# A fixed TensorE order for the second expert, with the output row blocks in late groups between its products

## The chip, the cores and the metric

The kernel runs on one core of one Trainium2 chip. The metric is the device time of one execution in microseconds (us). The kernel before took 958.3 us, the median of three runs (957.17 to 958.48).

The engines are named as the profile names them: PE is TensorE (matrix products), PEld its weight loads, DVE is VectorE, ACT is ScalarE, POOL is GpSimd, and SP is the queue that issues most of the transfers.

## The reference

Attention with two kinds of masks is followed by two experts. Only the second expert matters here:

```
a = x @ w_a          # x: 2304 x 512, w_a and w_b: 512 x 1536
b = x @ w_b
return a * b @ w_out # w_out: 1536 x 512
```

## The kernel before

Attention and the first expert fill the first 538 us. They leave the second expert's input in DRAM, in blocks named `x2d`. Everything below is about the second expert, which fills the rest.

**Precision.** Each operand is split in a high and a low part, and each product is three matmuls (high by high, high by low, low by high). `parts` makes such a split: ACT casts the high part (line 150), and DVE or POOL subtracts it to get the low part (line 151).

**Steps.** The list `steps` has 18 entries. A step takes one group g of 768 rows (three groups) and one pair p of the 1536 hidden columns' blocks (six pairs). The order is p = 0, 1, 2 for g = 0, then for g = 1, then for g = 2, and then the same with p = 3, 4, 5. Steps are counted from one below: the change begins with the fourth (i = 3), which is g = 1 with p = 0.

**Products of a step.** For each of `w_a` (k even) and `w_b` (k odd) the step makes a 2 by 2 block product with seven instead of eight block multiplications. `products` returns the seven as functions. Each is six matmuls of 384 columns into one of three PSUM banks, X, Y and Z. With both k there are 14 slots, in the order X0 X1 Y0 Y1 X0 X1 Y0 Y1 Z0 Z1 Y0 Y1 Z0 Z1 (the digit is k % 2). A product that stands a second or third time in the list accumulates onto what the bank holds, so it may only start when the engines have read the state before it: X0 is first copied by ACT (`u1`, line 872) and then accumulated onto, and Y0 is first added to `u1` by DVE (line 866).

**Hidden blocks.** `hidden` multiplies a and b (DVE, line 899) and splits the result into a tile `hl` (ACT line 150, POOL line 151).

**Output row blocks.** `output` multiplies hidden blocks with `wo2` into a PSUM tile `o`, and there are two such tiles. After a block, DVE adds it to an accumulator in SBUF (line 940), or ACT copies it there for the first pairs (line 938). A block has 12 matmuls of 512 columns when it serves two pairs, and six when it serves one. After each step with p % 3 of 1 or 2, six blocks are put on the list `waiting`. The next step takes one of them at every second slot.

**Other work in the same steps.** Steps three, five, six, eight and nine also convert weights (`convert_forms`): load `raw`, ACT lines 137 and 142, DVE line 145 writing `z`, sums `zs` (lines 680 to 683), casts and subtractions into the single tile `forms`, and a store to `formd`. The first three steps and the tenth to twelfth convert `wo2` in the same way, with the tiles `z2`. The scheduler may run such work in a neighbouring step. At the first step of each group `x_forms` rebuilds the seven split inputs in the tiles `slab`. The `form` tiles, which hold converted weights, are loaded a step ahead (line 807) into four buffers.

**What sets the order.** The code gives the order in which instructions are recorded. A scheduler then orders each engine's instructions by its own estimate of when each is ready. So PE's row order is not that of the code: it interleaves matmuls of several products and several output blocks. `behind(list)` forbids one thing to the scheduler: an instruction may not be put ahead of those in the list on its engine.

Of the kernel before, what the change touches and what calls it, by code (L numbers as in the profile page):

```python
# [77 lines left out]
def fused_kernel(ctx: ExitStack, tc: tile.TileContext, qtl, ktl, vl, qs, ks, vs, cst, w1, w2, out):  # L78
# [5 lines left out]
    nc = tc.nc  # L84
# [85 lines left out]
    def run(steps):  # L170
        for f in steps:
            f()
# [317 lines left out]
    def tmp(name):  # L490
        return act.tile([128, NTB], F32, tag="t", name=name, bufs=NTMP)
# [4 lines left out]
    @contextmanager  # L496
    def behind(instructions):

        with ExitStack() as e:
            for i in instructions:  # L500
                e.enter_context(tc.issue_after(i))
            yield
# [227 lines left out]
    for t in range(NB):  # L730
# [10 lines left out]
        x = [xt[t, cc] for cc in range(NCC)]  # L741
        for fc in range(NFC):
# [34 lines left out]
            if t == 0:  # L777
                nc.vector.tensor_tensor(v, sg, v, op=ALU.mult)
                h = v
                made[:] = [nc.vector.scalar_tensor_tensor(h, th, 1.0, v, op0=ALU.add, op1=ALU.mult).ins]  # L780
            else:
                h = tmp("h")
# [23 lines left out]
    def load_forms(k):  # L806
        nc.sync.dma_start(flat(form_tile(k)), formd[k])
# [3 lines left out]
    def convert_wo2(fc):  # L811
# [14 lines left out]
        def last():  # L826
            w = wo2[fc] = []
            for q in (2 * (fc % 6), 2 * (fc % 6) + 1):
# [7 lines left out]
    PRODUCTS = [(1, 0, "X", True), (6, 4, "Y", True), (2, 1, "X", False), (5, 3, "Y", False),  # L836
                (7, 6, "Z", True), (3, 5, "Y", False), (4, 2, "Z", False)]

    def part():
        return p2b.tile([128, NTB], F32, tag="c", name="c", bufs=8)  # L840

    def products(g, k):

        st = {}
        w = forms.pop(k)
        x = dict(xf)
        banks = {}

        def bank(n):
            return banks[n][:, :NTB]  # L850

        def product(p, form, n, begins):
            def f():
                if begins:
                    banks[n] = psum.tile([128, 512], F32, tag=f"{n}{k % 2}", name=f"{n}{k % 2}")
                for c in range(2):
                    cs = slice(c * 128, (c + 1) * 128)
                    hi, lo = w[:, 0, form, cs], w[:, 1, form, cs]
                    nc.tensor.matmul(bank(n), hi, x[p][:, 0, c], start=begins and c == 0, stop=False, skip_group_check=not begins)  # L859
                    nc.tensor.matmul(bank(n), hi, x[p][:, 1, c], start=False, stop=False, skip_group_check=not begins)  # L860
                    nc.tensor.matmul(bank(n), lo, x[p][:, 0, c], start=False, stop=c == 1, skip_group_check=not begins)  # L861
                after(p)
            return f

        def plus(dst, a, n):
            nc.vector.tensor_tensor(dst, a, bank(n), op=ALU.add)  # L866
            return dst

        def after(p):
            if p == 1:  # L870
                st["u1"] = part()
                nc.scalar.copy(st["u1"], bank("X"))
            elif p == 6:
                st["u2"] = plus(part(), st["u1"], "Y")
            elif p == 2:
                if k % 2 == 0:
                    st["11"] = part()
                    if (g, k) == (0, 0):
                        nc.vector.tensor_copy(st["11"], bank("X"))
                    else:  # L880
                        nc.scalar.copy(st["11"], bank("X"))
                else:
                    st["11"] = bank("X")
            elif p == 5:
                st["u4"] = plus(part(), st["u1"], "Y")
            elif p == 7:
                st["22"] = plus(st["u4"], st["u4"], "Z")
            elif p == 3:
                st["12"] = plus(st["u1"], st["u1"], "Y")
            elif p == 4:  # L890
                st["21"] = plus(st["u2"], st["u2"], "Z")

        return st, [product(*p) for p in PRODUCTS]
# [3 lines left out]
    def hidden(p, a, b, c):  # L897

        nc.vector.tensor_tensor(a[c], a[c], b[c], op=ALU.mult)  # L899
        h = hl[p, c] = p2c.tile([128, 2, NTB], F32R, tag="h", name="hl", bufs=9)  # L900
        parts(a[c], h[:, 0], h[:, 1], nc.gpsimd)
# [5 lines left out]
    def acc_tile(j):  # L907
        acc[j] = slab[j][:, 3 * DM:] if j < 2 else slab[11][:, (j - 2) * DM:(j - 1) * DM]
        return acc[j]

    def output(g, ps, j, last=False):

        t, cols = j // NJ, slice(j % NJ * 128, j % NJ * 128 + 128)
        r0 = (2 * g + t) * NTB + j % NJ * 128
        chunks = [(p, i) for p in ps for i in range(2)]
        if last:
            for half, queue in enumerate((nc.sync, nc.scalar)):
                c = slice(half * 256, half * 256 + 256)
                o = psum.tile([128, 512], F32, tag="o", name="o", bufs=2)[:, :256]
                for n, (p, i) in enumerate(chunks):  # L920
                    h, w = hl[p, f"{i + 1}{t + 1}"], wo2[2 * p + i]
                    nc.tensor.matmul(o, h[:, 0, cols], w[0][:, c], start=n == 0, stop=False)
                    nc.tensor.matmul(o, h[:, 0, cols], w[1][:, c], start=False, stop=False)
                    nc.tensor.matmul(o, h[:, 1, cols], w[0][:, c], start=False, stop=n == len(chunks) - 1)
                nc.vector.tensor_tensor(acc[j][:, c], acc[j][:, c], o, op=ALU.add)
                queue.dma_start(out[r0:r0 + 128, c], acc[j][:, c])
            return
        o = psum.tile([128, 512], F32, tag="o", name="o", bufs=2)
        for n, (p, i) in enumerate(chunks):
            h, w = hl[p, f"{i + 1}{t + 1}"], wo2[2 * p + i]  # L930
            nc.tensor.matmul(o, h[:, 0, cols], w[0], start=n == 0, stop=False)  # L931
            nc.tensor.matmul(o, h[:, 0, cols], w[1], start=False, stop=False)  # L932
            nc.tensor.matmul(o, h[:, 1, cols], w[0], start=False, stop=n == len(chunks) - 1)  # L933
        while reload and (reload[0][1] != j or len(reload) > 1):
            again = reload.pop(0)
            nc.sync.dma_start(acc_tile(again[1]), accd[again])
        if ps[0] == 0:
            nc.scalar.copy(acc_tile(j), o)
        else:
            nc.vector.tensor_tensor(acc[j], acc[j], o, op=ALU.add)  # L940
        if ps[-1] == NP // 2 - 1:
            nc.sync.dma_start(accd[g, j], acc[j])
            if g == NB // 2 - 1:
                reload.append((0, j))
        if ps[-1] == NP - 1:
            nc.sync.dma_start(out[r0:r0 + 128, :], acc[j])
            if g + 1 < NB // 2:
                reload.append((g + 1, j))


    steps = [(ps, g, p) for ps in (range(0, 3), range(3, 6)) for g in range(NB // 2) for p in ps]
    converted = {2: [6], 4: [7], 5: [8, 9], 7: [10], 8: [11]}
    wo_ready = {0: (0, 1), 1: (2, 3), 2: (4, 5), 9: (6, 7), 10: (8, 9), 11: (10, 11)}
    waiting = []
    for i, (ps, g, p) in enumerate(steps):
        if i > 0 and p == ps[0]:
            for fs in x_forms(g).values():
                run(fs)
        ahead = []
        if i + 1 < len(steps):  # L960
            for k in (2 * steps[i + 1][2], 2 * steps[i + 1][2] + 1):
                if k not in forms:
                    ahead.append(lambda k=k: load_forms(k))
        for fc in wo_ready.get(i, ()):
            ahead += convert_wo2(fc)
        for k in converted.get(i, ()):
            ahead += convert_forms(k, False, True)
        a, pa = products(g, 2 * p)
        b, pb = products(g, 2 * p + 1)
        slots = [f for fs in zip(pa, pb) for f in fs]  # L970
        for n, f in enumerate(slots):
            f()
            run(ahead[len(ahead) * n // 14:len(ahead) * (n + 1) // 14])
            if waiting and n % 2:
                waiting.pop(0)()
            if n in (7, 9, 11):
                hidden(p, a, b, {7: "11", 9: "22", 11: "12"}[n])
        hidden(p, a, b, "21")
        if p % 3:
            js = (*range(NJ, 2 * NJ), *range(NJ)) if i + 1 == len(steps) else range(2 * NJ)  # L980
            waiting += [lambda g=g, q=(p - 1, p) if p % 3 == 1 else (p,), j=j, last=i + 1 == len(steps) and j == js[-1]:
                        output(g, q, j, last) for j in js]
# [70 lines left out]
```

## Time and profile before

| | |
|---|---|
| median of three runs | 958.3 us |
| the profiled execution | 957.71 us |
| its span in the trace | 955.9 us |
| granted TensorE clock, mean over the span | 0.989 |
| TensorE busy | 931.4 us, 97% |
| VectorE, ScalarE, GpSimd busy | 66%, 44%, 56% |
| second expert in the trace | from 538.5 us to the end |
| first instruction that the change moves | TensorE, 601.80 us |

The span is what the trace covers, and the profiled execution's own time is 1.8 us longer. Times in the rows are us from the span's start.

### The profile page before, as it was taken

The numbers are of one execution on the slowest core, as the hardware profiler recorded it, in microseconds if no ns is written. First come the engines' busy times: TensorE is split into PE (matmuls) and PEld (weight loads), VectorE is DVE, ScalarE is ACT, GpSimd is POOL, SyncE is SP. The second block draws the span as 40 slices with busy tenths as digits, with TensorE's granted clock in tenths as the row PEclk, the third lists the DMA queues.
The fourth block names the chain that finished last, engine by engine and source line by source line (L and its number), as shares of the span: only waits on it lengthen the run. The fifth ranks groups of instructions, "written<-read, shape, count | busy, mean of one in ns | idle before, by whom it ended". The sixth has DMA issues, their size and how long they took to land.

```text
span 955.9 us, 14129 instructions
## 1 busy us (share of the span) xinstructions
PE 931.4 (97%) x5324; PEld 883.1 (92%) x5324; DVE 628.9 (66%) x916; ACT 420.7 (44%) x791; POOL 539.5 (56%) x405
## 2 busy tenths in 40 slices
PE   5999999999999999999999999999999999999998
PEld 3798899999999999999999998999999999999997
DVE  5669977558818895987576468667655655464534
ACT  5987645344443433444555545436424422122110
POOL 3568956468749687969379545655634424123211
PEclk6899999999999999999999999999999999999999
DMA  9974385527534553532787975997993973863701
GB/s 343 407 290 153 107 295 170 166 93 235 159 105 153 172 183 109 175 134 67 260 345 290 359 274 221 384 417 277 372 372 124 349 290 129 289 242 148 261 32 67
DMA packets 57507, 215.55 MB, mean 225 GB/s; under 512 B 5984, under 2 KB 14816, under 8 KB 51808
## 3 DMA queue, kind: packets, MB, share of 16 engines
q1 hardware_dynamic: 57152, 214.00, 61.6%
q8 instruction: 42, 0.69, 0.3%
q10 hardware_dynamic: 288, 0.66, 0.2%
q14 instruction: 25, 0.20, 0.1%
HBM read 172.17 MB, written 42.47 MB: 225 GB/s over the span
## 4 chain that ended last, share of the span: by engine, by line
PE 67%; DMA 9%; POOL 8%; DVE 6%; issue 4%; ACT 4%; SPq 0%; POOLq 0%; DVEq 0%; ACTq 0%
PE o L933 5%; PE o L932 5%; PE o L931 5%; POOL prod L248 4%; PE Y L860 4%; PE Y L861 4%; PE Y L859 4%; DMA raw<-in_w 3%; DMA gv_raw<-in_w 3%; PE y L482 3%; PE g_ps L483 3%; PE y L481 3%; PE y L483 3%; PE g_ps L481 3%; PE g_ps L482 3%
## 5 line engine op out<-in xcount | busy, mean ns | idle before, releaser
L151 POOL TENSOR_TENSOR hl<-c,hl 128x384 fp32r<-128x384 f32 x72 | 77.2, 1072 | 183.8 <-ACT hl L150 177.2
L248 POOL TENSOR_TENSOR prod<-kv_t,qs_t 128x512 f32<-128x512 f32 (+12 forms) x57 | 106.8, 1897 | 20.8 <-DMA kv_t<-in_ks 14.6
L482 PE MATMUL y<-hl,wo 128*128 128x384 f32 x288 | 97.1, 341 | 3.4 <-DVE hl L507 2.4
L281 POOL TENSOR_TENSOR prod<-kv_t,S_t 128x512 f32<-128x512 f32 (+12 forms) x57 | 86.8, 1536 | 21.8 <-issue 8.2
L481 PE MATMUL v_ps<-xx,gv 128*128 128x384 f32 x288 | 97.1, 337 | 2.0 <-DVE sg L762 1.9
L481 PE MATMUL g_ps<-xx,gv 128*128 128x384 f32 x288 | 97.3, 338 | 0.9 <-DVE sg L766 0.9
L482 PE MATMUL v_ps<-xx,gv 128*128 128x384 f32 x288 | 97.6, 339 | 0.0
L483 PE MATMUL v_ps<-xx,gv 128*128 128x384 f32 x288 | 97.2, 338 | 0.0
L483 PE MATMUL g_ps<-xx,gv 128*128 128x384 f32 x288 | 96.9, 337 | 0.0
L482 PE MATMUL g_ps<-xx,gv 128*128 128x384 f32 x288 | 96.5, 336 | 0.0
L866 DVE TENSOR_TENSOR c<-c,Y 128x384 f32<-128x384 f32 x108 | 58.8, 550 | 56.0 <-PE Y L861 50.8
L483 PE MATMUL y<-hl,wo 128*128 128x384 f32 x288 | 94.0, 335 | 0.0
L284 DVE TENSOR_REDUCE xs_t<-prod 128x64 f32<-128x448 f32 (+17 forms) x57 | 85.7, 1518 | 11.1 <-POOL prod L281 10.0
L507 POOL TENSOR_TENSOR hl<-h,hl 128x384 fp32r<-128x384 f32 x58 | 62.9, 1084 | 49.1 <-ACT hl L506 49.0
L481 PE MATMUL y<-hl,wo 128*128 128x384 f32 x288 | 84.0, 342 | 1.8 <-ACT hl L506 1.8
L932 PE MATMUL o<-slab,hl 128*128 128x512 f32 x214 | 83.9, 393 | 0.0
L931 PE MATMUL o<-slab,hl 128*128 128x512 f32 x214 | 83.4, 390 | 0.0
L933 PE MATMUL o<-slab,hl 128*128 128x512 f32 x214 | 82.3, 394 | 0.0
L150 ACT CAST hl<-c 128x384 fp32r<-128x384 f32 x72 | 36.9, 513 | 102.8 <-DVE c L899 102.8
L860 PE MATMUL Y<-slab,form 128*128 128x384 f32 x216 | 72.4, 335 | 0.0
L861 PE MATMUL Y<-slab,form 128*128 128x384 f32 x216 | 72.4, 335 | 0.0
L859 PE MATMUL Y<-slab,form 128*128 128x384 f32 x216 | 72.4, 335 | 0.0
(150 smaller groups left out, 2462.1 us busy)
## 6 DMA issues: line engine op xcount, KB each, us to landing
form<-formd SPq DMA_DIRECT2D x32, 1792.0 KB, 10.5
wo<-wod SPq DMA_DIRECT2D x59, 512.0 KB, 4.0
raw<-in_w SPq DMA_DIRECT2D x40, 512.0 KB, 7.2
gv_raw<-in_w SPq DMA_DIRECT2D x32, 512.0 KB, 10.2
formd<-form SPq DMA_DIRECT2D x6, 1792.0 KB, 8.2
formd<-forms SPq DMA_DIRECT2D x6, 1792.0 KB, 12.6
slab<-x2d SPq DMA_DIRECT2D x24, 384.0 KB, 4.2
wod<-wo SPq DMA_DIRECT2D x12, 512.0 KB, 3.0
```

Of the source, the lines that this page charges most:

```text
L248: nc.gpsimd.tensor_tensor(pr, st["ks", g][:, :, :n, :], st["qs"][:, heads(g), mm:mm + 1, :].to_broadcast([128, G, n, D]), op=ALU.mult)
L281: st["pvm"] = nc.gpsimd.tensor_tensor(pr, st["vs", g][:, :, :n, :], st["S"][:, heads(g), mm, :n, None].to_broadcast([128, G, n, D]), op=AL ...
L284: st["pvr"] = nc.vector.tensor_reduce(st["xs"][:, mm, heads(g), :], pr.rearrange("p g n d -> p g d n"), axis=X, op=ALU.add)
L481: nc.tensor.matmul(out_ps, w_hi, x_hi, start=start, stop=False)
L482: nc.tensor.matmul(out_ps, w_hi, x_lo, start=False, stop=False)
L483: nc.tensor.matmul(out_ps, w_lo, x_hi, start=False, stop=stop)
L859: nc.tensor.matmul(bank(n), hi, x[p][:, 0, c], start=begins and c == 0, stop=False, skip_group_check=not begins)
L860: nc.tensor.matmul(bank(n), hi, x[p][:, 1, c], start=False, stop=False, skip_group_check=not begins)
L861: nc.tensor.matmul(bank(n), lo, x[p][:, 0, c], start=False, stop=c == 1, skip_group_check=not begins)
L931: nc.tensor.matmul(o, h[:, 0, cols], w[0], start=n == 0, stop=False)
L932: nc.tensor.matmul(o, h[:, 0, cols], w[1], start=False, stop=False)
L933: nc.tensor.matmul(o, h[:, 1, cols], w[0], start=False, stop=n == len(chunks) - 1)
```

## The change

`turn` holds the last matmul that was recorded, and `in_turn` records a function's instructions behind it. From the fourth step on, each product and each output block is recorded that way, so PE runs them whole and in the order of the code. The output blocks no longer stand at every second slot. With six blocks waiting they come in three pairs after slots 8, 10 and 12 (p % 3 of 0 or 1), or in two threes after slots 6 and 11 (6 and 13 in the last step). Slots count from zero. The first three steps keep the scheduler's order.

```diff
+    turn = []
+
+    def in_turn(f):
+
+        with behind(turn):
+            f()
+
...
-                    nc.tensor.matmul(bank(n), lo, x[p][:, 0, c], start=False, stop=c == 1, skip_group_check=not begins)
+                    turn[:] = [nc.tensor.matmul(bank(n), lo, x[p][:, 0, c], start=False, stop=c == 1, skip_group_check=not begins).ins]
...
-            nc.tensor.matmul(o, h[:, 1, cols], w[0], start=False, stop=n == len(chunks) - 1)
+            turn[:] = [nc.tensor.matmul(o, h[:, 1, cols], w[0], start=False, stop=n == len(chunks) - 1).ins]
...
+        groups = (8, 10, 12) if p % 3 < 2 else (6, 11) if i + 1 < len(steps) else (6, 13)
         for n, f in enumerate(slots):
-            f()
+            if i < 3:
+                f()
+            else:
+                in_turn(f)
             run(ahead[len(ahead) * n // 14:len(ahead) * (n + 1) // 14])
-            if waiting and n % 2:
-                waiting.pop(0)()
+            if i < 3:
+                if waiting and n % 2:
+                    waiting.pop(0)()
+            elif n in groups:
+                for o in waiting[:6 // len(groups)]:
+                    in_turn(o)
+                del waiting[:6 // len(groups)]
```

No instruction that computes or moves data is added or removed: on PE, DVE, ACT, POOL and SP the counts of these are the same in both programs. Line numbers behind the new function grow by seven (line 866 becomes 873, 940 becomes 947, and so on). Up to PE's row at 601.80 us, and the matching rows of the other engines, the two orders are the same.

The first place is PE in the fourth step, where the second product into X0 begins. Before, a row block's matmuls stand just in front of it, and the product is split:

```order
L859 MATMUL Y1_6210<-slab_5002,form_5915 128x384
L860 MATMUL Y1_6210<-slab_5002,form_5915 128x384
L861 MATMUL Y1_6210<-slab_5002,form_5915 128x384
L931 MATMUL o_6219<-slab_5392,hl_6038 128x512
L932 MATMUL o_6219<-slab_5392,hl_6038 128x512
L933 MATMUL o_6219<-slab_5392,hl_6038 128x512
L859 MATMUL X0_6174<-slab_5068,form_5904 128x384
L931 MATMUL o_6192<-slab_5392,hl_6149 128x512
```

Of the change, the same place on PE; the row block `o` is gone from it:

```order
L866 MATMUL Y1_6201<-slab_5002,form_5915 128x384
L867 MATMUL Y1_6201<-slab_5002,form_5915 128x384
L868 MATMUL Y1_6201<-slab_5002,form_5915 128x384
L866 MATMUL X0_6174<-slab_5068,form_5904 128x384
L867 MATMUL X0_6174<-slab_5068,form_5904 128x384
```

Between the last matmul of the step's first X1 and this first matmul of the second X0, 18 matmuls (12 of 384 columns, six of 512) stood before, and 12 of 384 columns stand now. In the same step the first two row blocks come after Z0, and the third, `o_6291`, stands behind Z1 and the third product into Y0.

The second place is DVE in the fourth step. Before, the additions of the first two row blocks (line 940) stand behind one write of `z`:

```order
L145 SCALAR_TENSOR_TENSOR z0_6574<-raw_6560,z0_6574 128x512
L940 TENSOR_TENSOR slab_4797<-slab_4797,o_6192 128x512
L940 TENSOR_TENSOR slab_4856<-slab_4856,o_6219 128x512
L899 TENSOR_TENSOR c_6234<-c_6234,X1_6183 128x384
L145 SCALAR_TENSOR_TENSOR z1_6599<-raw_6562,z1_6599 128x512
L866 TENSOR_TENSOR c_6257<-c_6181,Y0_6201 128x384
L680 TENSOR_TENSOR zs_6636<-z1_6599 128x256
```

Of the change, the same stretch on DVE, down to the addition of the second block:

```order
L906 TENSOR_TENSOR c_6216<-c_6216,X1_6183 128x384
L145 SCALAR_TENSOR_TENSOR z0_6560<-raw_6546,z0_6560 128x512
L873 TENSOR_TENSOR c_6230<-c_6181,Y0_6192 128x384
L873 TENSOR_TENSOR c_6240<-c_6190,Y1_6201 128x384
L873 TENSOR_TENSOR c_6230<-c_6230,Z0_6246 128x384
L145 SCALAR_TENSOR_TENSOR z1_6571<-raw_6548,z1_6571 128x512
L680 TENSOR_TENSOR zs_6594<-z1_6571 128x256
L947 TENSOR_TENSOR slab_4797<-slab_4797,o_6254 128x512
L681 TENSOR_TENSOR zs_6594<-zs_6594,z0_6560 128x256
L682 TENSOR_TENSOR z1_6571<-z0_6560,z1_6571 128x256
L947 TENSOR_TENSOR slab_4856<-slab_4856,o_6263 128x512
```

The first block's addition has moved behind the second write of `z` and behind the first sum.

The third place is ACT in the seventh step (g = 2, p = 0), around the two copies of X0 and X1 into `c`. Before:

```order
L150 CAST forms_7109<-z1_7067 128x256
L150 CAST slab_5330<-slab_4856 128x768
L137 ACTIVATE raw_7230<-raw_7230 128x512
L872 COPY c_6812<-X0_6805 128x384
L142 ACTIVATE z0_7255<-raw_7200 128x512
L150 CAST hl_6780<-c_6558 128x384
L872 COPY c_6821<-X1_6814 128x384
L142 ACTIVATE z1_7266<-raw_7230 128x512
L881 COPY c_6865<-X0_6805 128x384
```

Of the change:

```order
L142 ACTIVATE z0_7213<-raw_7186 128x512
L137 ACTIVATE raw_7202<-raw_7202 128x512
L945 COPY slab_5517<-o_6718 128x512
L142 ACTIVATE z1_7266<-raw_7202 128x512
L945 COPY slab_5517<-o_6732 128x512
L137 ACTIVATE raw_7457<-raw_7457 128x512
L150 CAST slab_5330<-slab_4856 128x768
L879 COPY c_6812<-X0_6805 128x384
L150 CAST hl_6780<-c_6544 128x384
L879 COPY c_6821<-X1_6814 128x384
L150 CAST forms_7308<-z0_7213 128x512
L150 CAST forms_7308<-z1_7266 128x256
```

The conversion has moved up: the first instruction on the next tile, `raw_7457`, stands ahead of both copies, and four casts into `forms` (two of them shown) stand behind them and ahead of the next copy of X0.

## Rows read from the trace of the kernel before

**Rows 1.** The page: busy time, share of the span, instructions.

```profile
PE 931.4 (97%) x5324; PEld 883.1 (92%) x5324; DVE 628.9 (66%) x916; ACT 420.7 (44%) x791; POOL 539.5 (56%) x405
```

**Rows 2.** Windows: stretch, its length, busy and count by engine, clock, DMA share, GB/s.

```profile
601.80:700.00 98.20, 98.20 (x517) 91.65 (x517) 66.31 (x96) 45.01 (x86) 61.16 (x53) 1.00 0.93 372
700.00:952.70 252.70, 252.63 (x1316) 234.17 (x1315) 136.94 (x223) 64.59 (x116) 71.23 (x59) 1.00 0.55 205
```

**Rows 3.** Waits of PE from 538 us to the end: us, times, longest.

```profile
PE X L859 <- DVE c L899: 0.4, 1, 0.4
```

**Rows 4.** Timeline of PE, 700 to 705.6 us: start, duration, operation.

```profile
700.16 0.33 PE L859 MATMUL Y<-slab,form 128*128 128x384 f32 x1
...
701.72 0.33 PE L859 MATMUL Z<-slab,form 128*128 128x384 f32 x1
...
702.24 0.39 PE L931 MATMUL o<-slab,hl 128*128 128x512 f32 x1
...
705.46 0.33 PE L859 MATMUL Y<-slab,form 128*128 128x384 f32 x1
```

**Rows 5.** One of the three `o` groups of PE, 601.8 to 952.7 us.

```profile
L932 PE MATMUL o<-slab,hl 128*128 128x512 f32 x190 | 74.5, 393 | 0.0
```

**Rows 6.** Timeline of PE at the first difference.

```profile
601.80 0.39 PE L931 MATMUL o<-slab,hl 128*128 128x512 f32 x1
```

**Rows 7.** Timeline of ACT in the fourth step.

```profile
603.56 0.48 ACT L872 COPY c<-X 128x384 f32<-128x384 f32 x1
...
612.59 0.68 ACT L142 ACTIVATE z<-raw 128x512 uint32<-128x512 uint16 x1 [2.23 <-POOL forms L151]
```

**Rows 8.** Timeline of PE around a wait of the fourth step.

```profile
612.27 0.34 PE L861 MATMUL Z<-slab,form 128*128 128x384 f32 x1
612.61 0.50 PE L931 MATMUL o<-slab,hl 128*128 128x512 f32 x1
612.95 0.39 PE L932 MATMUL o<-slab,hl 128*128 128x512 f32 x1
```

**Rows 9.** Timeline of DVE in the fourth step.

```profile
610.03 1.93 DVE L145 SCALAR_TENSOR_TENSOR z<-raw,z 128x512 uint32<-128x512 uint32 x1 [4.61 <-ACT z L142]
611.89 1.27 DVE L940 TENSOR_TENSOR slab<-slab,o 128x512 f32<-128x512 f32 x2
...
613.55 0.68 DVE L145 SCALAR_TENSOR_TENSOR z<-raw,z 128x512 uint32<-128x512 uint32 x1
...
614.61 0.93 DVE L680 TENSOR_TENSOR zs<-z 128x256 f32<-128x256 f32 x1
...
615.93 0.41 DVE L681 TENSOR_TENSOR zs<-zs,z 128x256 f32<-128x256 f32 x1
```

**Rows 10.** Timeline of POOL in the fourth step.

```profile
609.55 1.86 POOL L151 TENSOR_TENSOR forms<-zs,forms 128x768 fp32r<-128x768 f32 x1
611.35 1.21 POOL L151 TENSOR_TENSOR forms<-z,forms 128x256 fp32r<-128x256 f32 x1
```

**Rows 11.** Timeline of ACT around the start of the seventh step.

```profile
668.45 0.93 ACT L150 CAST forms<-z 128x512 fp32r<-128x512 f32 x2
...
670.32 0.84 ACT L150 CAST slab<-slab 128x768 fp32r<-128x768 f32 x1
671.06 0.68 ACT L137 ACTIVATE raw<-raw 128x512 f32<-128x512 f32 x1
671.63 0.46 ACT L872 COPY c<-X 128x384 f32<-128x384 f32 x1
```

**Rows 12.** Loads of raw issued between 654 and 658.5 us.

```profile
DMA to landing us min/median/max: 4.2/5.6/7.0
```

**Rows 13.** Stores of formd issued between 600 and 700 us.

```profile
DMA to landing us min/median/max: 8.0/13.3/14.2
```

**Rows 14.** The tile form: its loads.

```profile
DMA to landing us min/median/max: 6.4/10.2/14.8
```

## The prediction

> **What bounds the kernel now.** I read the page first. PE is busy for 97% of the span, and no other engine is above 66% [rows 1]. A busy PE may still be waiting between its matmuls, so the windows come next. From 601.80 us, where the orders part, to PE's last matmul at 952.7 us PE is busy for 98.20 of 98.20 us and 252.63 of 252.70 us at the full granted clock, 2.4 GHz [rows 2]. The waits agree: in the whole second expert the only wait listed is 0.4 us [rows 3], and it comes in the first three steps, which don't change.
>
> A busy share can hide slack inside the rows, so I count starts. From 700.16 to 701.72 us nine matmuls of 384 columns start, one each 0.1735 us or so. From 702.24 to 705.46 us 14 of 512 columns start, one each 0.230 us [rows 4]. The two windows hold 1833 matmuls [rows 2]. Three lines of 190 make 570 of 512 columns [rows 5], 12 belong to the split last block (estimated at 0.12 us each), and about 1250 have 384 columns. 570 x 0.230 + 1250 x 0.1735 + 12 x 0.12 is 349.4 us, against 350.9 us elapsed. So all waits of PE that a better order could remove here come to about 1.5 us. One is visible: at 612.27 us the next matmul starts 0.34 us later instead of 0.17, and the one after it 0.34 instead of 0.23 us later [rows 8]. It costs 0.17 + 0.11 = 0.28 us, where the 0.11 is a restart that I add to each wait below. It ends 0.04 us after DVE's first addition of a block ends (611.89 + 0.68, half of the row of two and the gap) [rows 9], so 0.04 us is the way from an engine to PE.
>
> **What the change does.** It adds and removes no work. Per engine the counts of computing and moving instructions are the same, so the sum has waits alone as terms. Since PE has no idle time that could take a wait up, each new wait is added to the end in full. A product takes 6 x 0.1735 = 1.04 us, a block 2.76 us (12 matmuls) or 1.38 us (six).
>
> In a step without row blocks each bank has slack: three products, 3.12 us, lie between the end of the first X0 and the second X0, and ACT's copy needs 0.48 us [rows 7] plus the matmul's own tail. It is hidden as long as ACT is free. I looked for places where a neighbour engine is late and the scheduler's order gave PE something else to do.
>
> Place A, fourth step. The second X0 needs the copy that ends at 603.56 + 0.48 = 604.04 us [rows 7]; all of ACT's order up to there is unchanged. Before, 18 matmuls lie in between. Now PE is through its 12 matmuls from 601.80 us [rows 6] at 603.88 us. It waits until 604.08 us: 0.20 + 0.11 = **0.3 us**.
>
> Place B, same step. The third row block needs the PSUM tile of the first, so it needs the first's addition on DVE. PE wants it at 604.08 + 0.11 + 5 products (5.20) + two blocks (2.76) + Z1 and Y0 (2.08) = 614.23 us. The addition stands behind the second write of z. That waits for ACT's line 142 at 612.59 to 613.27 us [rows 7], and this for POOL's last piece of forms, which ends at 612.56 us [rows 10]. None of these depends on what moved. Then come the write of z (0.68 us, begun about 613.4 because three additions stand before it), the sum zs (0.93, of which some 0.08 overlaps the next) and the addition (0.68) [rows 9]: 614.1, 614.95, 615.65 us. PE starts at 615.7: 1.45 + 0.11 = **1.6 us**. The lower bound takes the sum at 0.41, the row of its sister, and gives 1.0. The upper bound lets the write of z take 1.93 as the one before it did [rows 9], and gives 2.8. That write of 1.93 us ended about half a us after POOL's piece of 609.55 + 1.86 us [rows 10]. The Trainium skill ("SBUF — State Buffer", Who interferes with whom) says that a DVE instruction with two SBUF inputs and a GpSimd instruction that reads SBUF block each other out for a whole instruction; the two rows fit it. By it the second write here would wait for at most one POOL piece of 1 us, giving 2.6 us for this place.
>
> Place C, seventh step. It starts at 599.72 + 22.85 (14 products, six short blocks) + 1.9 (A and B) + 14.57 + 31.13 (six long blocks) = 670.2 us, and wants its second X0 at 674.3. ACT now has the first work on a new raw tile ahead of the copy of X0. From the landing of that raw it takes 0.57 + 0.74 + 0.48 + 0.04 = 1.8 us to free the bank, by the spacing of the same operations [rows 11]. The load is issued when the z before it is written. That follows a cast that waits for the sixth step's third Y1 at about 659.9 us, then the forms casts (1.87) and five more ACT instructions: z's ACT part ends near 665.0 and DVE's write near 665.7 to 667.2 (0.68 to 1.93). Loads in front of which no form load stands landed after 4.2 to 7.0 us [rows 12], so this raw lands at 669.9 to 674.2, and PE gets the bank at 671.7 to 676.0: a wait of 0 to 1.8 us. The middle gives none; I take **0.4**.
>
> Behind these copies stand four casts that need the single forms tile back, so they wait for its store (8.0 to 14.2 us [rows 13], issued about 668.5). ACT's next copy of X0 follows them, DVE's product waits for that copy, and DVE's additions for the third row block (wanted near 685) queue behind it, some 2.8 us after the copy. A store of 8 to 11 us is hidden; 14.2 us costs about 2. I take **0.3**. DVE's additions behind B have 0.2 us to spare and could be hit by one more long DVE row: **0.2**.
>
> Transfers: the form loads keep their places within a row or two among the accumulator stores. The tightest is the second for the sixth step, issued at 624.8 when the last Z1 of the fourth has read its buffer, needed at 640.1; the longest landing is 14.8 us [rows 14], so it still arrives, with 0.5 us to spare. The tail is unchanged: the same seven blocks end the program, and three blocks now stand between the last Z1 and them.
>
> Sum: 0.3 + 1.6 + 0.4 + 0.3 + 0.2, less the 0.28 of before's own wait, is 2.5 us. The profiled execution took 957.7 us, so 960.2; the median of the runs lies 0.6 above it, so I predict **960.8 us**.
>
> **Rivals.**
> The waits are longer: the raw and the forms store of place C land late, together up to 3.8, and B takes 2.8. That is 0.3 + 2.8 + 3.8 + 0.2 - 0.3, about 7 us: 965. For it: stores and loads of that size do take 13 us where form loads compete [rows 13, 14]. Against it: here the form loads come behind them.
>
> The waits are absorbed: the engines run ahead of the rows of before because whole groups free them earlier, B shrinks to below 1 us and C is nothing. 958 to 959. For it: PE is the only full engine. Against it: the chain of B begins with rows that the change leaves as they are.
>
> It gets faster, by one mechanism: matmuls in whole groups start at shorter distances. The place is all of the stretch. If each of 570 came at 0.226 instead of 0.230 and each of 1250 at 0.1725, 2.3 + 1.2 = 3.5 us come off. It decides once it beats the 2.5 of the waits by 2, at 4.5 us: 956. Against it: in rows 4 runs of one kind already have the distances with which I counted, and the whole surplus is 1.5 us. The Trainium skill ("Perfetto Trace Analysis", Identifying the Most-Contended Engine) warns that matmul busy time is a poor measure of headroom, and would use the weight loads' busy share. That share is 234.17 of 252.70 us, 93% [rows 2]; by this rule 7% of the stretch, some 25 us, could come off, to 933. I weigh it low: the loads' free share is what a 512-column matmul leaves, since its distance of 0.230 us is longer than that of a 384-column one, and the order can't change that.
>
> **Numbers.** 0.2%, about 1.9 us, is what a measurement of this kernel can tell from no change. Forecast (waits of 1 to 4 us net) 0.58; longer waits 0.14; absorbed 0.18; denser matmuls 0.10. Of the forecast's 0.58 some 0.36 lies above 1.9 us. So slower 0.36 + 0.14 = 0.50, faster 0.10, and the same 0.40. The range runs from 957.2, most of the absorbed case, to 964.8, most of the long one; the likeliest case's own is 959.3 to 962.3.
>
> **What would show it.** Right: PE's waits list, empty before, has an o on a DVE addition near 614 us with 1.0 to 2.8 us and an X on an ACT copy near 604 us with 0.2; perhaps another X near 674 us. PE's rows keep 0.1735 and 0.230 us. Steps without row blocks have no wait. Wrong: distances that shrink, waits in the steady steps of the second half (after 770 us), where I see none, or a form that lands after PE wants it.

## The result and the profile after

The changed kernel takes **965.8 us**, the median of six runs (962.19 to 968.76). The kernel before took 958.3 us on the same chip, the median of six (957.17 to 959.80). The ratio is 1.007, with a 95% interval of 1.0053 to 1.0088: slower, by more than I forecast. The profiled execution took 962.86 us and its span is 961.1 us, against 957.71 and 955.9 us before.

The two pairs of numbers differ: 7.5 us between the medians, 5.2 us between the spans. The second expert alone, from the start of the first X matmul to the end of PE's last, gives 538.64 to 952.73 us before and 538.28 to 957.88 us after: **414.1 and 419.6 us, a loss of 5.5 us**. What the medians show above that seems to lie ahead of the second expert. In both of these profiles the granted clock is 1.00 from 30 to 100 us. A second profile of the changed kernel (below) has 0.94 and 0.96 there (30 to 60 and 60 to 100 us) and begins the second expert at 541.27 us, 3 us later; its span is 963.8 us, but its second expert takes 419.3 us. The twelve profiles of this document agree: the second expert begins at 538.0 to 539.3 us in the seven whose mean granted clock is 0.989 or more, and at 540.1 to 541.7 us in the five with 0.986 or less. So I measure by the second expert's length and quote medians beside it. That length is read from one profile of each version, and it has noise of its own: a wait in the first three steps, where no version but convlate changes the code, is listed with 0.2 to 0.9 us in the eleven others.

The page first, PE's row, which answers to [rows 1]:

```profile
PE 930.6 (97%) x5324; PEld 881.8 (92%) x5324; DVE 632.8 (66%) x916; ACT 421.4 (44%) x791; POOL 540.9 (56%) x405
```

No engine has more instructions than before; DVE is busy 3.9 us longer. The windows of the changed kernel (stretch, its length, busy time and count by engine, granted clock, DMA share, GB/s) answer to [rows 2]:

```profile
601.80:700.00 98.20, 95.57 (x499) 88.18 (x499) 64.48 (x95) 44.78 (x87) 60.82 (x53) 1.00 0.94 377
700.00:800.00 100.00, 100.00 (x530) 93.84 (x529) 59.29 (x91) 36.91 (x63) 34.30 (x28) 1.00 0.62 237
800.00:958.00 158.00, 154.87 (x804) 142.54 (x802) 84.29 (x134) 28.50 (x53) 38.23 (x32) 1.00 0.47 174
```

The clock is full in all three. PE, which had no idle time, now has 2.63 us in the first and 3.13 us in the last. The waits of PE from 538 us to the end (total, times, longest) answer to [rows 3]:

```profile
PE o L938 <- DVE slab L947: 4.0, 3, 1.5
PE X L866 <- ACT c L879: 0.9, 1, 0.9
PE o L938 <- ACT slab L945: 0.7, 1, 0.7
PE X L866 <- DVE c L906: 0.5, 1, 0.5
```

The last row is the wait of the first three steps that before has too. The rest is new: three times a row block waits for DVE's addition, once a block for ACT's copy out of PSUM, once a second X0 for ACT's copy. Here are five of the six places on PE (start, duration, operation, and in brackets the idle time and what ended it):

```profile
603.36 0.34 PE L868 MATMUL Y<-slab,form 128*128 128x384 f32 x1
603.71 0.44 PE L866 MATMUL X<-slab,form 128*128 128x384 f32 x1
...
613.71 0.34 PE L868 MATMUL Y<-slab,form 128*128 128x384 f32 x1
615.09 0.50 PE L938 MATMUL o<-slab,hl 128*128 128x512 f32 x1 [1.04 <-DVE slab L947]
...
651.04 0.39 PE L940 MATMUL o<-slab,hl 128*128 128x512 f32 x1
652.14 0.50 PE L938 MATMUL o<-slab,hl 128*128 128x512 f32 x1 [0.71 <-ACT slab L945]
...
674.51 0.34 PE L868 MATMUL Y<-slab,form 128*128 128x384 f32 x1
675.72 0.45 PE L866 MATMUL X<-slab,form 128*128 128x384 f32 x1 [0.87 <-ACT c L879]
...
803.61 0.39 PE L940 MATMUL o<-slab,hl 128*128 128x512 f32 x1
805.46 0.50 PE L938 MATMUL o<-slab,hl 128*128 128x512 f32 x1 [1.47 <-DVE slab L947]
805.80 0.39 PE L939 MATMUL o<-slab,hl 128*128 128x512 f32 x1
```

The bracket understates a wait, because a matmul's row runs past the start of the next. Read starts instead. 805.46 is 1.85 us behind 803.61 where 0.23 is usual, and the matmul after it starts 0.34 us later, again 0.11 too much. So each place costs the late start and the restart. From 603.36 on the six are 0.28, 1.31, 0.97, 1.14, 1.73 and, at 873.88 us, 1.73 us: **7.2 us in all**. Before's own wait of 0.28 us is gone [rows 8]. Matmuls elsewhere came a little closer. The mean distance of neighbours of one width, waits left out, went from 174.3 to 173.9 ns for 384 columns and from 230.2 to 228.7 ns for 512, and over 1248 and 570 matmuls that is 0.5 + 0.9 = 1.4 us. 7.2 - 0.3 - 1.4 = 5.5 us, as measured.

The two largest waits stand in the twelfth and fifteenth step, at places where I had seen none. DVE shows why. Its timeline in the twelfth step:

```profile
797.47 0.55 DVE L873 TENSOR_TENSOR c<-c,Z 128x384 f32<-128x384 f32 x1
797.93 0.55 DVE L873 TENSOR_TENSOR c<-c,Y 128x384 f32<-128x384 f32 x1
798.39 1.69 DVE L717 TENSOR_TENSOR slab<-slab 128x768 f32<-128x768 f32 x1
800.00 2.19 DVE L906 TENSOR_TENSOR c<-c 128x384 f32<-128x384 f32 x1
802.12 0.54 DVE L873 TENSOR_TENSOR c<-c,Y 128x384 f32<-128x384 f32 x1
802.59 0.94 DVE L151 TENSOR_TENSOR slab<-slab 128x768 fp32r<-128x768 f32 x1
803.46 1.35 DVE L906 TENSOR_TENSOR c<-c 128x384 f32<-128x384 f32 x1
804.73 1.27 DVE L947 TENSOR_TENSOR slab<-slab,o 128x512 f32<-128x512 f32 x2
```

And POOL's beside it:

```profile
797.38 1.88 POOL L151 TENSOR_TENSOR slab<-slab 128x768 fp32r<-128x768 f32 x1 [10.40 <-ACT slab L150]
799.47 2.32 POOL L151 TENSOR_TENSOR slab<-slab 128x768 fp32r<-128x768 f32 x1 [0.21 <-ACT slab L150]
802.89 1.50 POOL L151 TENSOR_TENSOR hl<-c,hl 128x384 fp32r<-128x384 f32 x1 [1.11 <-ACT hl L150]
```

This step ends a group, so `x_forms` builds the next group's inputs in it and three of its subtractions run on POOL. The two rows of L906 (the product in `hidden`) are the same operation on the same shape; undisturbed it takes 0.55 us. Each ends 0.4 us after a POOL row does: POOL at 799.47 + 2.32 = 801.79, DVE at 802.19; POOL at 804.39, DVE at 804.81. The subtraction L717 ahead of them takes 1.69 us where it takes 0.95 undisturbed. So the first block's addition begins at 804.73 us. PE, through the first block at 801.11 and the second at 803.84, has waited since for the first one's PSUM tile.

### The profile page after: what moved, and what is told of

It reads as the page before. It is cut to its first block, busy times and chain, and to the rows that moved or that the text cites. A ratio compares the mean times of both kernels' runs of the same rounds, so it can differ in the third digit from the quotient of the medians.

```text
span 961.1 us, 14144 instructions
## 1 busy us (share of the span) xinstructions
PE 930.6 (97%) x5324; PEld 881.8 (92%) x5324; DVE 632.8 (66%) x916; ACT 421.4 (44%) x791; POOL 540.9 (56%) x405
## 4 chain that ended last, share of the span: by engine, by line
PE 58%; DMA 12%; DVE 10%; POOL 9%; issue 5%; ACT 5%; SPq 0%; DVEq 0%; POOLq 0%; ACTq 0%
POOL prod L248 4%; PE o L938 4%; PE o L940 4%; PE o L939 4%; DMA raw<-in_w 3%; PE Y L868 3%; DMA gv_raw<-in_w 3%; PE Y L866 3%; PE Y L867 3%; PE y L482 3%; PE g_ps L483 3%; PE y L481 3%; PE y L483 3%; PE g_ps L481 3%; PE g_ps L482 3%
## 5 line engine op out<-in xcount | busy, mean ns | idle before, releaser
L873 DVE TENSOR_TENSOR c<-c,Y 128x384 f32<-128x384 f32 x108 | 59.3, 550 | 60.2 <-PE Y L868 54.4
```

## The experiments

**My theory** after reading the trace: the loss is PE's waits and nothing else, and the two of 1.73 us come from groups of three blocks with only two PSUM tiles. The third wants the first's tile after one block, 2.76 us, while DVE is held by POOL. **The rivals**: (a) the fixed order in itself costs, wherever the blocks stand; (b) the moved weight conversion costs; (c) the loss lies ahead of the second expert and isn't the change's.

**again**: the changed kernel once more, nothing edited.

> The changed kernel unchanged, run again on this chip beside the others. It is the measure for them: a second profile tells which of PE's waits come back at the same place. Theory one (a row block's PSUM tile or bank X is freed late by VectorE or ScalarE, at fixed places of the order): the same waits near 604, 614, 651, 674, 804 and 874 us, each within 0.7 us of the first profile, 7 us together, and a time of 962 to 967 us. Rival theory (the loss changes from run to run: transfers or the clock at the start): waits at other places, or the same waits with a time that moves by more than 3 us.

965.58 us beside 958.64 us before, ratio 1.0061 (1.0043 to 1.0079); second expert 419.3 us. All six waits come back at the same places, with 0.66, 1.33, 0.83, 0.82, 1.73 and 1.73 us. Those of the first half move by some tenths from run to run, the two of the second half not at all. Rival (c) is out as the main cause.

**pairs**: no threes but in the last step.

```diff
-        groups = (8, 10, 12) if p % 3 < 2 else (6, 11) if i + 1 < len(steps) else (6, 13)
+        groups = (8, 10, 12) if i + 1 < len(steps) else (6, 13)
```

> The steps that took the six row blocks in two threes take them in three pairs after slots 8, 10 and 12; the last step keeps its threes. Theory one: the third block of a three wants the first's PSUM tile back only 2.76 us after the first ends, which VectorE misses; pairs with products between them give it 4.8 us or more. The waits near 651 (1.0 us), 804 and 874 us (1.7 us each) go, those near 604, 614 and 674 us stay: 4.4 us less than the changed kernel, so some 961 us. Rival (waits come from whole products in a fixed order, whatever the grouping): no change within 1 us.

959.04 us, ratio 1.0006 (0.9990 to 1.0022); second expert 414.7 us. The waits of PE:

```profile
PE o L938 <- DVE slab L947: 0.8, 1, 0.8
...
PE Y L866 <- DVE c L873: 0.3, 1, 0.3
```

Both large waits are gone, and those at 651 and 674 us too. What is left is 0.28 at 605 us, 1.07 at 616 us, and two new ones of 0.55 and 0.21 us at a Y (647, 716 us). The fixed order stays, and almost all of the loss goes. Rival (a) is out.

Two things in this run were not expected. The wait at 674 us went too, and the kernel took 959.04 us, not 961. The scheduler had ordered DVE and ACT anew around the pairs. In the twelfth and fifteenth step no held product is left in front of an addition (each takes 0.56 us), so this run doesn't separate the distance between the blocks from DVE's queue. In the seventh step ACT copies X0 before its first work on the raw tile, which lands late here too:

```profile
672.97 0.48 ACT L879 COPY c<-X 128x384 f32<-128x384 f32 x1 [0.20 <-PE X L868]
...
675.27 0.68 ACT L137 ACTIVATE raw<-raw 128x512 f32<-128x512 f32 x1 [0.79 <-DMA raw<-in_w]
```

**single**: six groups of one block each.

```diff
-        groups = (8, 10, 12) if p % 3 < 2 else (6, 11) if i + 1 < len(steps) else (6, 13)
+        groups = (5, 6, 8, 9, 11, 12)
```

> Fixed order as in the change, but the row blocks one at a time, after slots 5, 6, 8, 9, 11 and 12 in every step. Theory one: a tile is wanted back at least one block and two products after its block ends, so no row block waits for VectorE, also not near 614 us: about 5.5 us less than the changed kernel, some 960 us, unless the earlier blocks find their hidden block not split yet (a wait on hl, up to 1 us a step). Rival (fixed order as such): no change within 1 us.

962.14 us, ratio 1.0018 (0.9999 to 1.0036); second expert 417.1 us. Its waits:

```profile
PE X L866 <- DVE c L906: 0.8, 1, 0.8
PE o L938 <- DVE slab L947: 0.8, 1, 0.8
PE X L866 <- DMA form<-formd: 0.4, 1, 0.4
PE o L940 <- POOL hl L151: 0.2, 1, 0.2
```

Both large waits are gone here too. My expectation of 960 us missed, and so did the one for 614 us: that wait stays, with 1.06 us at 615.4 us. And two new ones come: a form that lands late (0.67 us) and a block that wants a `hl` that isn't ready (0.46 us). Spreading blocks is not free.

**free**: the groups of the change, but the scheduler may order PE.

```diff
-            if i < 3:
-                f()
-            else:
-                in_turn(f)
+            f()
...
-                for o in waiting[:6 // len(groups)]:
-                    in_turn(o)
+                run(waiting[:6 // len(groups)])
```

> The grouping alone: products and row blocks are recorded in the change's places, but nothing fixes TensorE's order, so the scheduler interleaves as before. Theory one: the scheduler moves matmuls into the places where a tile is late by its own estimate, so the waits shrink below 2 us in sum: 957 to 960 us. If the grouping as such cost the time, it would stay near 965 us.

959.21 us, ratio 1.0000 (0.9988 to 1.0012); second expert 413.8 us. Only 0.24 and 0.42 us of waits are left, near 616 and 618 us. So the groups alone cost nothing that shows either: the loss needs both, a bank that comes free late and a PE that may not do something else meanwhile.

**nolow**: in the last three groups POOL leaves out its subtractions in `x_forms` (`once` is true from the tenth step's inputs on), so three of the seven inputs keep an old low part.

```diff
+        once = len(built) >= 3 * 7
...
-            parts(src, f[:, 0], f[:, 1], nc.gpsimd if p in (3, 4, 7) else nc.vector)
+            if once and p in (3, 4, 7):
+                nc.scalar.copy(f[:, 0], src)
+            else:
+                parts(src, f[:, 0], f[:, 1], nc.gpsimd if p in (3, 4, 7) else nc.vector)
+            built.append(p)
```

> The change, but where the last three groups' inputs are rebuilt (x_forms for the tenth, thirteenth and sixteenth step) GpSimd's three subtractions are left out, so three of the seven inputs keep an old low part; VectorE's order is the same row for row. Theory lock (VectorE's two-input rows are held until GpSimd's subtraction ends, and the row block's addition stands behind them): the rows of 2.2 and 1.35 us near 800 and 870 us shrink to 0.55, the addition ends 2.4 us earlier, and both waits of 1.7 us go; the second expert takes 416.0 instead of 419.5 us. Rival (VectorE is late by the number of its rows alone): the waits stay above 1 us.

960.63 us, ratio 1.0014 (0.9994 to 1.0034); second expert 416.7 us. Both waits of 1.73 us are gone; the four of the first half are still there (0.54, 1.46, 0.98, 0.82 us). DVE's timeline in its twelfth step, with the same order of rows:

```profile
799.58 0.95 DVE L725 TENSOR_TENSOR slab<-slab 128x768 f32<-128x768 f32 x1
800.45 0.55 DVE L914 TENSOR_TENSOR c<-c 128x384 f32<-128x384 f32 x1
...
802.25 1.37 DVE L914 TENSOR_TENSOR c<-c 128x384 f32<-128x384 f32 x1
803.54 0.68 DVE L955 TENSOR_TENSOR slab<-slab,o 128x512 f32<-128x512 f32 x1
```

The first product takes 0.55 us where it took 2.19; the second, beside which POOL's `hl` subtraction still runs, is still held at 1.37. The subtraction ahead of both takes 0.95 us where it took 1.69. So two DVE rows are shorter, by 1.64 and 0.74 us, and a wait whose late start was 1.62 us is gone. PE's order and its threes are those of the change. This is the run that shows POOL's hold on DVE as the cause of the two large waits.

The Trainium skill ("SBUF — State Buffer", Who interferes with whom) says that DVE and GpSimd share a pair of SBUF ports, locked for whole instructions. The trace agrees: 2.19 us beside POOL, 0.55 without it.

**convlate**: the first ACT work on a converted `wo2` tile is recorded behind the latest copy of X.

```diff
+    copied = []
...
-            st["words"][0]()
+            with behind(copied):
+                st["words"][0]()
...
-                nc.scalar.copy(st["u1"], bank("X"))
+                copied[:] = [nc.scalar.copy(st["u1"], bank("X")).ins]
```

> The change, but the first ScalarE work on a raw tile of w_out is recorded behind the latest copy of X, so in the seventh step no work on a raw tile stands ahead of the two copies. Theory one: the wait of 0.8 to 1.1 us near 674 us goes, and nothing else moves before 700 us. Rival (the copy is late for another reason, such as the cast into slab before it): a wait of at least 0.5 us stays there. The conversions now crowd into the tenth to twelfth step, which may cost up to 2 us near 740 to 800 us.

968.19 us in two runs, ratio 1.0091 (1.0059 to 1.0123); second expert 423.7 us. A miss. The wait at 674 us falls to 0.51 us, from 1.14 and 0.82 in the two profiles of the change, instead of going. The two largest groups of PE's waits:

```profile
PE o L940 <- DVE slab L949: 5.0, 4, 1.6
PE X L868 <- DMA form<-formd: 3.8, 2, 3.0
```

Two forms now land late, and one holds PE for 3.26 us at 710 us. What made them late was not tested. The waits of 1.73 us are untouched. At 674 us the copy of X0 is still late, because ACT has another conversion row ahead of it:

```profile
674.22 0.67 ACT L142 ACTIVATE z<-raw 128x512 uint32<-128x512 uint16 x1 [2.07 <-POOL forms L151]
```

With pairs the conversion's rows either end early (L142 at 669.29 us) or come behind the copy, and the wait is gone. So the rows speak for rival (b) at this one place. No run moved the conversion alone and removed the wait, so it is not shown, and holding the conversion back is no cure.

**from10**: fixed order and groups from the tenth step on only, where POOL's `x_forms` still stands but the waits of the first half can't.

```diff
-            if i < 3:
+            if i < 9:
...
-            if i < 3:
+            if i < 9:
```

> The fixed order and its groups from the tenth step on instead of the fourth. Theory one: the first nine steps have before's waits (0.3 us), and of the change's waits the two near 804 and 874 us are left (3.5 us); with the slightly closer matmuls of the change (estimated 0.7 us for this half) the second expert takes 414.1 - 0.7 + 3.5 = 416.9 us. Rival (the waits follow from the order in the first half, which shifts the later steps against GpSimd): no waits above 0.5 us, 413.5 us.

961.36 us, ratio 1.0021 (1.0004 to 1.0038); second expert 416.6 us, 0.3 below what was expected. The waits on DVE's additions:

```profile
PE o L938 <- DVE slab L947: 2.9, 2, 1.5
```

The two of 1.73 us alone (801.2 and 871.4 us), and before's own at 612 us. So the loss of 5.5 us splits in two: 2.5 from these (two waits less the closer matmuls), 3 from the first half.

**pairs10**: the same, without threes but in the last step (both edits above).

> The fixed order from the tenth step on, with pairs in place of the threes except in the last step. Theory one: no wait of TensorE is left but those of before, and the closer matmuls bring 0.7 us: the second expert takes 413.4 us and the kernel 957.6, not to be told from before. Rival (whole products cost something that is no wait): above 414.1 us.

958.34 us, ratio 0.9998 (0.9985 to 1.0011); second expert 413.7 us, with 413.4 expected. Nothing is left but a wait of 0.42 us near 613 us, where before has one of 0.28.

**gap1**: from10, but in the steps with threes one product stands between the second and the third block.

```diff
-        groups = (8, 10, 12) if p % 3 < 2 else (6, 11) if i + 1 < len(steps) else (6, 13)
+        groups = {8: 2, 10: 2, 12: 2} if p % 3 < 2 else {6: 2, 7: 1, 11: 2, 12: 1} if i + 1 < len(steps) else {6: 3, 13: 3}
...
-                for o in waiting[:6 // len(groups)]:
+                for o in waiting[:groups[n]]:
...
-                del waiting[:6 // len(groups)]
+                del waiting[:groups[n]]
```

> As the kernel with the fixed order from the tenth step on, but one product (1.04 us) stands between the second and the third block of each three. Theory lock: VectorE's addition ends when it did, and the tile is wanted 1.04 us later, so each of the two waits near 801 and 871 us falls from 1.73 to some 0.7 us with its restart; the second expert takes 414.6 us. Rival (the wait moves along with the block, since the addition is late by its own place in VectorE's order): 416.6 us as without the product.

957.85 us beside 957.81 us before, ratio 0.9992 (0.9965 to 1.0018); second expert 413.9 us, with 414.6 expected. There is no wait left in the twelfth and fifteenth step. It was not a pure test of the distance, because the scheduler ordered DVE anew as well:

```profile
800.98 1.62 DVE L906 TENSOR_TENSOR c<-c 128x384 f32<-128x384 f32 x1
802.53 0.68 DVE L947 TENSOR_TENSOR slab<-slab,o 128x512 f32<-128x512 f32 x1
```

The addition stands behind two held products as in the change, but they take 1.55 (at 798.93 us) and 1.62 us, and the subtraction L717 is no longer held. It ends at 803.21 us, and PE is through the second block only at 804.66 us. So the tile was free before the added product began: DVE's order removed the wait here, and the distance was not tested.

**lowdve**: from10, but in the last three groups DVE makes those three subtractions.

```diff
-            parts(src, f[:, 0], f[:, 1], nc.gpsimd if p in (3, 4, 7) else nc.vector)
+            late = len(built) >= 3 * 7
+            parts(src, f[:, 0], f[:, 1], nc.gpsimd if p in (3, 4, 7) and not late else nc.vector)
+            built.append(p)
```

> As the kernel with the fixed order from the tenth step on, but the three subtractions of the inputs' low parts for the last three groups run on VectorE, not on GpSimd; everything is computed. Theory lock: VectorE's rows are no longer held, but two more rows of 0.87 us stand ahead of the first block's addition, which then ends 1.2 us earlier than with GpSimd: two waits of 0.4 to 0.6 us, 414.2 us for the second expert. Rival (VectorE's load alone): the waits grow by 1.7 us each, to 420 us.

957.66 us, ratio 1.0002 (0.9973 to 1.0031); second expert 414.4 us, with 414.2 expected. DVE has more to do and still frees the tile in time: its two products by `hidden` there take 0.55 and 0.78 us instead of 2.19 and 1.35. The scheduler also moved the first addition ahead of the second product, so the hold is not the only thing that changed. No wait is left in the twelfth step and 0.63 us in the fifteenth. Part of what this won is given back near 612 us, where the wait that before has too is 0.91 us here.

No version beats the kernel before by more than its interval. pairs, pairs10, gap1, free and lowdve can't be told from it.

Threes cost nothing by themselves. The last step of the change still has them. No inputs are rebuilt there, so none of POOL's long subtractions runs, and DVE stands idle until PE ends a block. PE's waits list has nothing in that step:

```profile
928.41 0.69 DVE L947 TENSOR_TENSOR slab<-slab,o 128x512 f32<-128x512 f32 x1 [2.14 <-PE o L940]
```

In the twelfth step the tile comes back 4.35 us after its block ends (801.11 to 805.46 us). That is more than the 2.76 us that a three leaves and less than the 4.8 us of a pair with two products behind it. So a pair should cover even a held DVE; this is worked out from the rows, and no run has a pair behind the same held rows.

## Why the prediction was wrong, point by point

**No idle time to win, and each new wait lands in the end: right.** The sum of waits, less the closer matmuls, explains the 5.5 us.

**Place A, 0.3 us: right.** 0.28 us measured, and 0.3 to 0.7 in the other runs with the fixed order at that place.

**Place B, 1.6 us: right, a little too large.** 1.31 us. The rows came as argued, but the sum `zs` took 0.42 and not 0.93 us. About half of that was given back ahead of it: the write of `z` took 0.79 and not 0.68 us and ended 0.2 us later against PE than I had it. DVE at that place in the changed kernel:

```profile
613.18 0.79 DVE L145 SCALAR_TENSOR_TENSOR z<-raw,z 128x512 uint32<-128x512 uint32 x1
614.01 0.42 DVE L680 TENSOR_TENSOR zs<-z 128x256 f32<-128x256 f32 x1
614.35 0.68 DVE L947 TENSOR_TENSOR slab<-slab,o 128x512 f32<-128x512 f32 x1
```

**Place C, 0.4 us: right mechanism, too small.** 1.14 us here and 0.82 in the second profile, inside the 0 to 1.8 I had worked out. ACT sat idle for a raw tile that landed late in that span, with the copy queued behind it:

```profile
673.90 0.68 ACT L137 ACTIVATE raw<-raw 128x512 f32<-128x512 f32 x1 [2.80 <-DMA raw<-in_w]
674.48 0.81 ACT L150 CAST slab<-slab 128x768 fp32r<-128x768 f32 x1
675.20 0.47 ACT L879 COPY c<-X 128x384 f32<-128x384 f32 x1
```

**The store of the forms behind C (0.3) and near misses of DVE (0.2): neither came as described.** No wait follows C before 803 us.

**The step that failed** is the search for places, which ended with "waits in the steady steps of the second half (after 770 us), where I see none". I found late neighbours in the fourth and seventh step alone, and so put at nothing the waits in the sixth, twelfth and fifteenth: 0.97 + 1.73 + 1.73 = 4.4 us. It failed at two points.

First, I didn't count from one block to the next but one inside a group. A three wants the first block's tile back after 2.76 us. In before the scheduler puts other matmuls between the blocks.

Second, I priced DVE's rows there at their undisturbed length, although I had used POOL's hold for place B. By the rows above two held rows of 2.19 and 1.35 us instead of 0.55 each come to 2.4 us, and the 1.69 instead of 0.95 of the subtraction to 0.7 more: 3.2 us, more than the wait. Without them, by these rows, the addition would have ended near 802.2 us, before PE wanted the tile at 803.84.

The ninth step of the changed kernel is the control. Its DVE rows are held just as long, and PE doesn't wait there:

```profile
731.50 2.20 DVE L906 TENSOR_TENSOR c<-c 128x384 f32<-128x384 f32 x1
...
734.96 1.36 DVE L906 TENSOR_TENSOR c<-c 128x384 f32<-128x384 f32 x1
```

The blocks of that step are those of the first pairs, which ACT copies out of PSUM; no addition queues behind the held rows.

The wait at 651 us is the same fault at ACT. A three's blocks are copied by ACT there, whose queue has a conversion ahead of the copies, and that waits for POOL:

```profile
650.95 0.67 ACT L142 ACTIVATE z<-raw 128x512 uint32<-128x512 uint16 x1 [1.38 <-POOL forms L151]
651.51 1.06 ACT L945 COPY slab<-o 128x512 f32<-128x512 f32 x2
```

That removing the threes removes this wait is shown by pairs, where that conversion still stands ahead of the first copy (652.38 us). That the conversion in front of it is what made the copy late is read from these rows, not tested by a run of its own.

**The rivals.** Of "the waits are longer" the median came out at its time (965), but by luck. It gave the waits 7 us where the second expert lost 5.5, what lies ahead of the second expert made up the rest, and the places were wrong: at B and C the waits were not as long as it had them, and there were more of them elsewhere. "Denser matmuls" was real, with 1.4 of the 3.5 us that I gave it, and too small to decide. The weight loads' share, which would have left 25 us to win, gave nothing: it is 93.84 of 100.00 us in the windows after, with PE at 100.00.

**From the profile to the median** I added 0.6 us; it was 3 us, because three of these six runs had a mean granted clock of 0.984 instead of 0.989 or more and took 965.6 to 966.8 us; the slowest run, 968.76 us, had 0.991, and for it no cause was found. By the second expert's length the change costs 5.5 us where I said 2.5.

## What to carry to other kernels

Before fixing an order on a full engine, walk through it bank by bank: for each PSUM tile the time from its last write to its next first write, against the queue in front of the instruction that frees it, with each row of that queue at its contended length. A group one larger than the number of tiles turns a slack of several products into that of one block. That is enough while the engine that frees the tile stands ready, as in the last step here, and too little when its queue is held. Versions with groups of two and two tiles lost almost nothing here. A scheduler that may interleave hides such waits, so a trace of it that shows none says nothing about a fixed order.

## What the runs showed of the hardware

DVE instructions with two SBUF operands were held while POOL subtracted: a 0.55 us product lasted 2.19 us beside a POOL subtraction of 2.32 us, while two DVE additions with an operand in PSUM (L873 at 797.47 and 797.93 us) kept their 0.55 us beside a POOL subtraction that began at 797.38 us and lasted 1.88. The whole second expert of the changed kernel bears this out: 89 rows of L873 overlap a POOL row and none lasts over 0.56 us, while 32 rows of L906 with both operands in SBUF last 0.56 to 2.21 us beside one. With POOL's subtractions moved onto DVE, the busier engine, the path that PE waited on was shorter. And each of PE's restarts after a wait cost about 0.1 us more on the next matmul (0.10 to 0.12), in every profile, after waits of 0.1 as of 3 us.
